# Block 0 of a feed-forward layer: second products of four more column tiles in three parts, and the low parts of five first weights made later, on VectorE

## The chip, the cores and the metric

The kernel runs on one core of a Trainium2 chip. The metric is the device time of one execution in microseconds (us): 551.14 for the kernel before, the median of three runs (551.05 to 551.84). Engines are named as in the profile: PE is TensorE (matmul), PEld its weight loads, DVE VectorE, ACT ScalarE, POOL GpSimd, and SP SyncE, whose queue issues most DMA transfers.

## What is computed

Three stages follow each other on 1536 tokens (2 batches of 768) of width 512. The change lies in the second.

```python
x = attention(q, k, v)                   # 8 heads of 64, window of 128 and 4 sink keys
h = x @ w_in                             # [1536, 512] @ [512, 2048]: the first products
g = np.maximum(0.01 * h, h)              # leaky ReLU
y = g @ w_out                            # [1536, 2048] @ [2048, 512]: the second products
...                                      # then a mixture of 8 experts, one per token
```

The weights `w_in` and `w_out` arrive as float64 and are turned into float32 on the chip, word by word.

## The kernel before, in words

**Blocks and column tiles.** The feed-forward layer takes the tokens in six blocks of 256 (two query tiles of 128 each), and the 2048 columns of `w_in` in 16 column tiles `f` of 128. For one block `j` and column tile `f`, `FFN.first` multiplies 128 columns of `w_in` with the block's `x` (`hps`, L1101), `FFN.leak` applies the leaky ReLU, and `FFN.second` adds `g` times 128 rows of `w_out` into two PSUM tiles `y`, one for each query tile (L1149). A product is written as a pair of column tile and kind: (f, 0) for the first weights, (f, 1) for the second.

**Two ways to multiply.** A product is made either of plain float32 operands, or "in parts": each operand is split into a rounded high part (ACT casts it: `wh` L1046, `gp` L1129) and the low rest (a subtraction on POOL or DVE: `wl` L1047, `gp` L1131), and three products are added: high by high, high by low, low by high. `FFN.in_parts` says which: every block after block 0 works in parts, and in block 0 the column tiles from `AHEAD[0]` (first products) and `AHEAD[1]` (second products) on. Before, `AHEAD = (5, 10)`.

**Block 0.** While block 0 runs, the weights are still arriving. Each column tile of weights is loaded by SP (`rawi`, `rawo`), and DVE converts it in three instructions (L1018 and L1022 write `word`, L1028 writes `cvt`, in pairs of column tiles). First all 16 first products run, then the second products of column tiles 0 to 13 (`LAG = 2`: the last two run in block 1). Attention for the following query tiles is woven between them. For a column tile in parts the function `ready` prepares the second product two column tiles ahead: the leaky ReLU's subtraction on POOL if it was put off (`gr` L1114, put off for `f >= LATE_G`), the split of the weights (`wh` on ACT, `wl` on POOL), the split of `g` (`gp` on ACT, then on POOL).

**Weights that block 0 used plain** must be split before block 1 needs them. The list `splits` holds them. Before, block 0 splits the first weights (f, 0) of column tiles 0 to 4 on POOL, one after each second product, and block 1 splits the ten second weights (f, 1) on DVE, `SPLIT = 1` for each column tile.

**What sets the order.** PE, SP, ACT, POOL, and up to the end of block 0 DVE too, keep the order in which the program issues their instructions; nothing is moved past a waiting instruction. Where DVE's conversions stand between other work is set by a planner (`Pace`), which compares its own sums of PE and DVE time (`pace.tensor`, `fill`). Tiles live in a pool of 70 slots, so an instruction that writes into a slot also waits for the last reader of the tile that held it.

**Saved weights.** The parts of column tiles 0, 1, 14 and 15 are written to a scratch buffer in HBM (`wscr`, L1057, on SP's queue) and read back in later blocks.

```python
def in_parts(self, j, f, x):
    return j > 0 or f >= self.ahead[x]
...
            self.late[f] = lambda: nc.gpsimd.tensor_tensor(out=g, in0=g, in1=r, op=ALU.subtract)
            if f < LATE_G:
                self.late.pop(f)()
```

Of the kernel before, what the change touches and what calls it, by code (L numbers as in the profile page):

```python
# [40 lines left out]

RAW = 5
LAG = 2
SPLIT = 1
LATE_G = 4
SLACK = 1.5
AHEAD = (5, 10)
WORD_US = 0.6
PARTS_US = 2.0
AFTER = range(9, 16)  # L50
# [901 lines left out]
class FFN:  # L952
# [12 lines left out]
    def __init__(self, nc, pools, A, xt, cap):  # L965
# [6 lines left out]
        self.w, self.v, self.raw, self.g, self.y = {}, {}, {}, {}, {}  # L972
        self.ahead, self.x0 = AHEAD, []
        self.seq = [(0, 0), (0, 1)] + [(f, x) for x in range(2) for f in range(1, self.NF)]
# [129 lines left out]
    def leak(self, j, f):  # L1104
# [3 lines left out]
        if j == 0:  # L1108
# [5 lines left out]
# [3 lines that stand above are left out]
# [898 lines left out]
def build(tc, A, n_sink, window, capacity):  # L2015
    nc = tc.nc
# [13 lines left out]
    with ExitStack() as es:  # L2030
# [34 lines left out]
        def step(*between):  # L2065

            nonlocal done
            d, pre, mid = steps.pop(0) if steps else (None, (), ())
            for f in (*pre, *between, *mid):
                f()  # L2070
            if d is not None:
                done = d
# [6 lines left out]
        if ring:  # L2079
# [3 lines left out]
            ffn = FFN(nc, p, A, xt, FFN.CAP)  # L2083
# [13 lines left out]
        if not ring:  # L2097
            pool(rawst, "raw", bufs=nraw, side="right")
            ffn = FFN(nc, p, A, xt, FFN.CAP - FEWER // 4)
# [18 lines left out]
        def some(calls, n):  # L2118
            for f in calls[:n]:
                f()  # L2120
            del calls[:n]
# [12 lines left out]
        def word():  # L2134

            if not conv:
                if chunk >= len(ffn.seq):
                    return False
                conv.extend(convert())
            f = conv.pop(0)  # L2140
            f()
            pace.dve += f.us
            if f.key:
                pace.ready[f.key] = pace.dve
            return True

        def fill():

            while started and pace.dve < pace.pe + SLACK and word():
                pass  # L2150
# [3 lines left out]
        def need(f, x):  # L2154

            while x not in ffn.v.get(f, ()) and x not in ffn.w.get(f, ()):
                word()
# [19 lines left out]
        pending, held, routing, splits, beside = [], [], [], [], []  # L2177
# [17 lines left out]
        def split(n, f=-1, x=0):  # L2195

            while splits and (n > 0 or f >= 0 and x not in ffn.w.get(f, ())):
                ffn.split(*splits.pop(0), nc.vector if ffn.phase > 1 else nc.gpsimd)
                n -= 1

        def second():
            j, f, i = pending.pop(0)
            if j == 0:
                need(f, 1)
                pace.tensor(*(1.4, (f, 1), PARTS_US) if ffn.in_parts(0, f, 1) else (1.88, (f, 1)))
            if j == 1:
                split(0, f, 1)
            last = i == ffn.NF - 1
            if j == late and i >= ffn.NF - HOLD:

                ffn.second(j, f, i == 0, last, range(TPB - 1))
                held.append((j, f, i))
                if last:
                    for t in range(TPB - 1):
                        rt.evac(j * TPB + t, ffn.y[j][t])
                return
            ffn.second(j, f, i == 0, last, range(TPB))
            del ffn.g[j, f]
            if j == 0:
                splits.extend([(f, 1)] * (not ffn.in_parts(0, f, 1)))  # L2220
            elif i < n_ev or j == late:
                del ffn.w[f]
            if j > 1 and i < n_ev:
                ffn.reload(ffn.order(j)[ffn.CAP + i])
            if last:
                ts = tuple(range(j * TPB, (j + 1) * TPB))
                for t, y in zip(ts, ffn.y.pop(j)):
                    rt.evac(t, y)
                routing.extend(route(ts, True) if j < late - 1 else late_route(ts))
                if j == late - 2 and rt.NU:  # L2230
                    routing.insert(-1, ex.rank)

        def ready(f):

            if f < ffn.NF:
                need(f, 1)
                if f in ffn.late:
                    ffn.late.pop(f)()
                if ffn.in_parts(0, f, 1):
                    ffn.split(f, 1, nc.gpsimd)  # L2240
                ffn.split_g(0, f)

        def block0():

            NF, last_t, ndone = ffn.NF, 2 * TPB - 1, 0
            pace.pe, pace.dve = 0.0, 1.7
            count = next((n + 1 for n, x in enumerate(steps) if x[0] == last_t), len(steps))
            for s in range(2 * NF - LAG):
                x, f = divmod(s, NF)
                if x == 0:  # L2250
                    need(f, 0)
                    ffn.first(0, f)
                    pace.tensor(*(1.42, (f, 0), PARTS_US) if ffn.in_parts(0, f, 0) else (1.95, (f, 0)))
                    if not ffn.in_parts(0, f, 0):
                        splits.append((f, 0))
                    ffn.leak(0, f)
                    if f == 0 and ffn.ahead[0] < NF:
                        ffn.split_x0()
                    fill()
                    for a in range(f + 2 if f else 0, f + 3):  # L2260
                        if ffn.ahead[0] <= a < NF:
                            need(a, 0)
                            ffn.split(a, 0, nc.gpsimd)
                    if f == NF - 1:
                        while conv:
                            word()
                        ffn.phase = 1
                        for a in range(LAG):
                            ready(a)
                else:  # L2270
                    pending.append((0, f, f))
                    second()
                    fill()
                    if f + LAG < NF - 1:
                        ready(f + LAG)
                    if splits and not splits[0][1]:
                        split(1)
                while ndone < min(count, max(1, count * (s + 1) // (2 * NF - LAG - 1))):
                    step()
                    ndone += 1  # L2280
                fill()
            while word():
                pass
            pending.extend((0, f, f) for f in range(NF - LAG, NF))
            ffn.store()
            ffn.phase = 2

        started = 1
        block0()
        order.close()  # L2290
        psc.close()
# [11 lines left out]
        for j in range(1, NB):  # L2303
# [14 lines left out]
            for i, f in enumerate(ffn.order(j)):  # L2318
# [10 lines left out]
                if (j, i) == (1, 0):  # L2329
                    ready(ffn.NF - 1)  # L2330
# [6 lines left out]
                while more():  # L2337
                    step()
                    ndone += 1
                split(SPLIT)  # L2340
                some(clears, rate)
# [87 lines left out]
```

## Time and profile before

| what | before |
| --- | --- |
| median of three runs | 551.14 us (551.05 to 551.84) |
| the profiled execution: its own time | 551.71 us |
| the profiled execution: its span, first to last instruction | 550.0 us |
| PE busy | 533.1 us, 97% of the span |
| DVE busy | 394.2 us, 72% |
| ACT busy | 291.6 us, 53% |
| POOL busy | 210.7 us, 38% |
| mean granted TensorE clock | 0.995 |

Busy time is an average over stages with different limits. Where an engine is nearly always busy, the question at each place is whether it waits, and for whom; where it is often idle, it can still be the one that the next step waits for. The rows for that stand in the section on rows; all lengths of time in them are us, except the mean of one instruction, in ns.

### The profile page before, as it was taken

Reading aid. Unit: us, or ns where it says so; the run is one execution under the profiler, and the core shown is the slowest. Engines: PE = TensorE matmul, PEld = TensorE weight load, DVE = VectorE, ACT = ScalarE, POOL = GpSimd, SP = SyncE. Lnnn points to the kernel's source line nnn. Section 1 sums busy time; section 2 is a strip of 40 time slices with the busy share of each in tenths; the row PEclk is TensorE's granted clock in tenths of the full one; section 3 lists DMA queues with packets and bytes.
Section 4 is the critical chain, followed back from the end, with each engine's and each line's share of the span. In section 5 each row is a group of like instructions: output and inputs, shape, how many; then the busy total and the mean of one; then the engine's idle time right before and its main releaser. Section 6 shows DMA issues by size and latency. Waiting matters only on the chain.

```text
span 550.0 us, 11107 instructions
## 1 busy us (share of the span) xinstructions
PE 533.1 (97%) x3653; PEld 457.9 (83%) x3653; DVE 394.2 (72%) x935; ACT 291.6 (53%) x858; POOL 210.7 (38%) x338
## 2 busy tenths in 40 slices
PE   8998999999999999999999999999999999999993
PEld 7777756888888888888888889888798988988782
DVE  5999996657439974898469952394587667838991
ACT  5768647765444454545454433373255545527771
POOL 6567579713525533553444552241110110102120
PEclk9999999999999999999999999999999999999998
DMA  9979873999564022420240037673376876747920
GB/s 226 243 226 283 258 268 99 360 276 324 170 225 116 21 57 66 129 56 22 68 128 28 1 113 237 217 228 124 99 215 214 254 243 191 241 130 227 348 81 7
DMA packets 83668, 93.72 MB, mean 170 GB/s; under 512 B 42963, under 2 KB 51155, under 8 KB 83472
## 3 DMA queue, kind: packets, MB, share of 16 engines
q1 hardware_dynamic: 81680, 87.78, 53.1%
q0 software_dynamic: 1920, 5.13, 2.6%
q8 instruction: 31, 0.51, 0.4%
q14 instruction: 37, 0.30, 0.2%
HBM read 74.10 MB, written 19.83 MB: 171 GB/s over the span
## 4 chain that ended last, share of the span: by engine, by line
PE 69%; DVE 14%; issue 8%; DMA 4%; POOL 2%; ACT 2%; POOLq 0%; ACTq 0%; DVEq 0%
PE y L1149 19%; PE hps L1101 19%; PE ph L1669 9%; PE py L1726 8%; DVE junk L1255 3%; DMA out<-ys,gt 3%; DVE word L1018 3%; PE ops L714 3%; DVE word L1022 2%; PE sps L618 2%; PE py L1732 1%; DVE cvt L1028 1%; DMA rawo<-in_moe_w_out 1%; PE pps L676 1%; DVE pm L628 1%
## 5 line engine op out<-in xcount | busy, mean ns | idle before, releaser
L1149 PE MATMUL y<-wh,gp 128*128 128x512 f32 x344 | 126.3, 408 | 0.2 <-POOL gp L1131 0.2
L1131 POOL TENSOR_TENSOR gp<-g,gp 128x256 fp32r<-128x256 f32 x77 | 68.0, 883 | 147.0 <-ACT gp L1129 124.8
L1101 PE MATMUL hps<-xth,wh 128*128 128x256 f32 x320 | 90.8, 284 | 0.0
L1101 PE MATMUL hps<-xtl,wh 128*128 128x256 f32 x320 | 90.4, 282 | 0.0
L1101 PE MATMUL hps<-xth,wl 128*128 128x256 f32 x320 | 90.0, 281 | 0.0
L1498 DVE TENSOR_TENSOR cw<-craw,cw 128x512 fp32r<-128x512 f32 x128 | 82.6, 690 | 4.4 <-ACT cw L1496 1.9
L1120 DVE TENSOR_TENSOR g<-hps,g 128x256 f32<-128x256 f32 x80 | 33.5, 419 | 60.9 <-ACT g L1119 60.7
L1149 PEld LDWEIGHTS y<-wh,gp 128*128 128x128 f32 x344 | 64.5, 188 | 14.7 <-POOL gp L1131 0.9
L1496 ACT CAST cw<-craw 128x512 fp32r<-128x512 f32 x112 | 63.5, 622 | 17.6 <-PE py L1732 9.2
L1149 PE MATMUL y<-wl,gp 128*128 128x512 f32 x172 | 67.6, 393 | 0.0
L1255 DVE SCALAR_TENSOR_TENSOR junk<-x,rows_of 128x512 f32<-128x512 f32 x48 | 62.9, 1311 | 1.2 <-ACT x L1227 1.0
L1101 PEld LDWEIGHTS hps<-xth,wh 128*128 128x128 f32 x320 | 60.3, 189 | 3.1 <-issue 0.4
L1101 PEld LDWEIGHTS hps<-xtl,wh 128*128 128x128 f32 x320 | 60.2, 188 | 2.7
L1119 ACT ACTIVATE g<-hps 128x256 f32<-128x256 f32 x80 | 30.5, 381 | 59.8 <-PE hps L1101 56.7
L1101 PEld LDWEIGHTS hps<-xth,wl 128*128 128x128 f32 x320 | 60.7, 190 | 0.0
L1726 PE MATMUL py<-cw,ht 128*128 128x512 f32 x216 | 53.7, 400 | 0.2 <-DVE ht L1714 0.2
L1129 ACT CAST gp<-g 128x256 fp32r<-128x256 f32 x80 | 32.7, 409 | 33.1 <-DVE g L1120 31.9
L1669 PEld LDWEIGHTS ph<-xt,cw 128*128 128x128 f32 x396 | 49.5, 189 | 0.7 <-issue 0.3
L1669 PE MATMUL ph<-xt,cw 128*128 128x256 f32 (+3 forms) x396 | 49.8, 287 | 0.1
L1726 PEld LDWEIGHTS py<-cw,ht 128*128 128x128 f32 x216 | 39.7, 188 | 9.4 <-DVE ht L1714 1.0
L1742 POOL DMA_INDIRECT out<-ys,gt x9 | 9.7, 1081 | 92.5 <-DVE ys L1741 92.5
L641 ACT ACTIVATE pm<-pm,mx 128x132 f32<-128x132 f32 (+1 forms) x80 | 31.8, 401 | 25.1 <-DVE mx L633 25.1
(264 smaller groups left out, 1024.6 us busy)
## 6 DMA issues: line engine op xcount, KB each, us to landing
craw<-in_moe_w SPq DMA_DIRECT2D x128, 256.0 KB
rawi<-in_moe_w_in SPq DMA_DIRECT2D x16, 512.0 KB
rawo<-in_moe_w_out SPq DMA_DIRECT2D x16, 512.0 KB
places<-zero SPq DMA_DIRECT2D x24, 257.0 KB
wh<-wscr SPq DMA_DIRECT2D x16, 256.0 KB
wl<-wscr SPq DMA_DIRECT2D x16, 256.0 KB
natv<-in_v SPq DMA_DIRECT2D x12, 256.0 KB
out<-zero SPq DMA_DIRECT2D x12, 256.0 KB
```

What stands on the lines that cost most here:

```text
L641: self.nc.scalar.activation(a, a, AF.Exp, bias=mx[:, pr, e:e + 1], accum_out=su[:, pr, e, 0:1])
L1101: nc.tensor.matmul(ps, lhsT=w, rhs=x, start=(n == 0), stop=(n == len(mm) - 1))
L1119: nc.scalar.activation(g, ps, AF.Copy, scale=0.01)
L1120: nc.vector.tensor_tensor(out=g, in0=ps, in1=g, op=ALU.max)
L1129: nc.scalar.copy(gp[:, 0], g)
L1131: eng.tensor_tensor(out=gp[:, 1], in0=g, in1=gp[:, 0].bitcast(F32), op=ALU.subtract)
L1149: nc.tensor.matmul(y, lhsT=l, rhs=r, start=(start and n == 0), stop=(stop and n == len(mm) - 1))
L1255: nc.vector.scalar_tensor_tensor(out=junk, in0=self.x2[ts[n]][:, 0:DM], scalar=1.0, in1=self.rows_of[:, :, e], op0=ALU.mult, op1=ALU.mult, ...
L1496: nc.scalar.copy(h, t)
L1498: eng.tensor_tensor(out=l, in0=t, in1=h.bitcast(F32), op=ALU.subtract)
L1669: nc.tensor.matmul(self.ph[f][:, sl], lhsT=self.w[e, "a", h, k][w][:, f * P:(f + 1) * P], rhs=self.xt[:, a, k, sl], start=(m == 0), stop=( ...
L1726: nc.tensor.matmul(self.py[n], lhsT=x, rhs=w, start=(h == 0 and f == 0 and m == 0), stop=(h == self.NH - 1 and f == self.HF - 1 and m == 2))
```

## The change

Five numbers and three places in the code:

- `AHEAD[1]` goes from 10 to 6: in block 0 the second products of column tiles 6 to 9 are made in parts too, so their weights and `g` are split in block 0 by `ready`.
- `LATE_G` goes from 4 to 9: the leaky ReLU's subtraction on POOL is put off for column tiles 9 to 15 alone; those of 4 to 8 follow their first products at once.
- Block 0 no longer splits first weights after its second products. At its end it splits two column tiles' (`EARLY_SPLITS = 2`) on DVE; block 1 splits the rest, two for each column tile (`SPLIT = 2`), ordered by when block 1 needs them.
- The second weights of column tile 15, prepared in block 1, get their low part on DVE and not on POOL.

```diff
-SPLIT = 1
-LATE_G = 4
+SPLIT = 2
+EARLY_SPLITS = 2
+LATE_G = 9
 SLACK = 1.5
-AHEAD = (5, 10)
+AHEAD = (5, 6)
...
                 if ffn.in_parts(0, f, 1):
-                    ffn.split(f, 1, nc.gpsimd)
+                    ffn.split(f, 1, nc.vector if ffn.phase > 1 else nc.gpsimd)
                 ffn.split_g(0, f)
...
                     if f + LAG < NF - 1:
                         ready(f + LAG)
-                    if splits and not splits[0][1]:
-                        split(1)
...
             ffn.store()
             ffn.phase = 2
+            splits.sort(key=lambda a: a[0] + LAG * a[1])
+            split(EARLY_SPLITS)
```

Three places of the built program show what moves. Line numbers of the changed kernel are one higher.

POOL's queue in the second half of block 0, before, from the masking of a probability tile (`pt`) on; `gr` is the leaky ReLU's subtraction, `wl` the low part of a weight tile, `gp` the low part of `g`, `pm` and `psk` scale attention's probabilities:

```order
L691 AFFINE_SELECT pt<-pt 128x512 x2
L1114 TENSOR_TENSOR gr<-gr 128x256 x3
L652 TENSOR_TENSOR pm<-pm,ri 128x528
L659 COPY psk_210<-pm 128x16
L1114 TENSOR_TENSOR gr<-gr 128x256
L1047 TENSOR_TENSOR wl<-cvt,wh 128x512
L1131 TENSOR_TENSOR gp<-gr,gp 128x256
```

The same place in the changed kernel, from the same `pt` to the same `gr`, `wl`, `gp`, which are those of column tile 10:

```order
L692 AFFINE_SELECT pt<-pt 128x512 x2
L1048 TENSOR_TENSOR wl<-cvt,wh 128x512
L1132 TENSOR_TENSOR gp<-gr,gp 128x256
L1048 TENSOR_TENSOR wl<-cvt,wh 128x512
L1132 TENSOR_TENSOR gp<-gr,gp 128x256
L1115 TENSOR_TENSOR gr<-gr 128x256
L1048 TENSOR_TENSOR wl<-cvt,wh 128x512
L1132 TENSOR_TENSOR gp<-gr,gp 128x256
L653 TENSOR_TENSOR pm<-pm,ri 128x528
L660 COPY psk_210<-pm 128x16
L1115 TENSOR_TENSOR gr<-gr 128x256
L1048 TENSOR_TENSOR wl<-cvt,wh 128x512
L1132 TENSOR_TENSOR gp<-gr,gp 128x256
```

Two `gr` (column tiles 7 and 8) have left this stretch, and three `wl` and three `gp` (column tiles 7, 8 and 9) have come into it. The rest of block 0 on POOL is the same in both: for column tiles 11, 12 and 13 `gr`, `wl`, `gp`, with two `pt` ahead of 13.

ACT's queue at the end of block 0 in the changed kernel, from the parts of column tile 14 on (`xth` is the high part of attention's result, `g` the first step of block 1's leaky ReLU):

```order
L1047 CAST wh<-cvt 128x512
L1130 CAST gp<-gr 128x256
L723 CAST xth<-ops 128x2x128
L1047 CAST wh<-cvt 128x512 x2
L1120 ACTIVATE g<-hps 128x256
```

Before, `g` follows `xth` at once. The two `wh` between them are those of the first weights of column tiles 0 and 1, with which block 1 begins. DVE's queue at the same place in the changed kernel:

```order
L592 TENSOR_TENSOR kTl_132<-qps,kTh_131 128x2x128
L734 TENSOR_TENSOR xtl<-ops,xth 128x2x128
L1048 TENSOR_TENSOR wl<-cvt,wh 128x512 x2
L1121 TENSOR_TENSOR g<-hps,g 128x256
```

The two `wl` are the low parts of the same two weights; before, `g` follows `xtl`.

## Rows read from the trace of the kernel before

**Rows 1.** Four stretches of the span: busy time and instructions of each engine.

```profile
core 0: us, PE busy (x) PEld busy (x) DVE busy (x) ACT busy (x) POOL busy (x), PEclk, DMA share, GB/s
34.65:59.80 25.15, 21.34 (x175) 18.47 (x174) 25.05 (x53) 19.01 (x63) 17.84 (x18) 1.00 0.93 279
76.65:95.66 19.01, 18.83 (x112) 11.34 (x110) 14.84 (x32) 11.68 (x39) 16.46 (x22) 1.00 0.50 147
95.66:107.40 11.74, 11.69 (x80) 10.37 (x81) 7.43 (x18) 9.47 (x32) 8.91 (x13) 1.00 0.97 353
```

**Rows 2.** Chain that ended last, by time: start, us, engine, tile, line.

```profile
65.62 5.97 DMA rawo<-in_moe_w_out
...
94.93 0.74 POOL gp L1131
95.71 1.20 PE y L1149 x4
96.91 1.53 PE hps L1101 x12
...
111.18 1.36 PE y L1149 x6
```

**Rows 3.** PE's timeline; in brackets idle time before, and its releaser.

```profile
68.23 3.70 PE L1149 MATMUL y<-cvt,gr 128*128 128x512 f32 x8
71.86 0.39 PE L618 MATMUL sps<-kTh,qT 64*128 64x264 f32 x2
...
96.74 0.28 PE L1101 MATMUL hps<-xth,wh 128*128 128x256 f32 x1
...
98.16 0.28 PE L1101 MATMUL hps<-xth,wl 128*128 128x256 f32 x1
```

**Rows 4.** POOL's timeline in the second half of block 0.

```profile
76.65 1.23 POOL L691 TENSOR_SCALAR_AFFINE_SELECT pt<-pt 128x512 f32<-128x512 f32 x2 [0.48 <-ACT pt L688]
77.85 2.12 POOL L1114 TENSOR_TENSOR gr<-gr 128x256 f32<-128x256 f32 x3
82.44 1.07 POOL L652 TENSOR_TENSOR pm<-pm,ri 128x528 f32<-128x528 f32 x1 [2.48 <-DVE ri L650]
...
87.22 1.29 POOL L1047 TENSOR_TENSOR wl<-cvt,wh 128x512 fp32r<-128x512 f32 x1
88.47 0.73 POOL L1131 TENSOR_TENSOR gp<-gr,gp 128x256 fp32r<-128x256 f32 x1
89.17 0.73 POOL L1114 TENSOR_TENSOR gr<-gr 128x256 f32<-128x256 f32 x1
...
94.93 0.73 POOL L1131 TENSOR_TENSOR gp<-gr,gp 128x256 fp32r<-128x256 f32 x1
95.61 0.75 POOL L1114 TENSOR_TENSOR gr<-gr 128x256 f32<-128x256 f32 x1
```

**Rows 5.** ACT's timeline, around the same places.

```profile
76.96 0.64 ACT L697 ACTIVATE sp<-kps,of_pair 128x128 f32<-128x128 f32 x2
...
96.39 0.41 ACT L1129 CAST gp<-gr 128x256 fp32r<-128x256 f32 x1 [0.39 <-POOL gr L1114]
96.70 0.37 ACT L722 CAST xth<-ops 128x256 fp32r<-128x256 f32 x1
...
101.27 0.62 ACT L1046 CAST wh<-cvt 128x512 fp32r<-128x512 f32 x1
```

**Rows 6.** Low parts on DVE up to 130 us, as a group.

```profile
L1047 DVE TENSOR_TENSOR wl<-cvt,wh 128x512 fp32r<-128x512 f32 x8 | 7.1, 889 | 3.8 <-ACT wh L1046 3.7
```

**Rows 7.** Two of them in DVE's timeline.

```profile
101.92 1.20 DVE L1047 TENSOR_TENSOR wl<-cvt,wh 128x512 fp32r<-128x512 f32 x1 [0.95 <-ACT wh L1046]
...
105.46 0.69 DVE L1047 TENSOR_TENSOR wl<-cvt,wh 128x512 fp32r<-128x512 f32 x1 [0.81 <-ACT wh L1046]
```

**Rows 8.** POOL's timeline beside the first of the two.

```profile
101.83 0.75 POOL L1131 TENSOR_TENSOR gp<-gr,gp 128x256 fp32r<-128x256 f32 x1
102.53 1.20 POOL L1131 TENSOR_TENSOR gp<-g,gp 128x256 fp32r<-128x256 f32 x1
```

## The prediction, made before the changed kernel ran

> **What bounds the kernel now.** PE is busy 97% of the span, so the first question is where it waits. I read the stretches first, then the chain of waits, then the timelines of the engines named there.
>
> In the second half of block 0, from 76.65 to 95.66 us, PE is busy 18.83 of 19.01 us, which looks like a bound by PE; but POOL is busy 16.46 us there too, and its only long gap is 2.48 us ahead of the scaling `pm`, where it waits for DVE's `ri` [rows 1, 4]. The chain of waits says who is last at the end of that stretch: it comes from DVE and a late load (`rawo`), runs through POOL, and reaches PE at 95.71 with POOL's `gp`, the low part of column tile 13; from there on it is PE after PE [rows 2]. So at the end of block 0 PE and POOL finish almost together, POOL a little later. After that, from 95.66 to 107.40, PE is busy 11.69 of 11.74 us [rows 1]: nothing there takes up a delay, and what block 0 ends later, the kernel ends later. In the first half of block 0 DVE, with its conversions, is the bound: 25.05 of 25.15 us between 34.65 and 59.80 [rows 1].
>
> **The change, part by part.**
>
> *PE's work.* Two plain second products (column tiles 2 and 3) take from 68.23 to 71.86, 1.81 us for each [rows 3]; one in parts takes 1.36 us on the chain [rows 2]. Four column tiles change over: 4 x (1.81 - 1.36) = 1.8 us less work for PE. It counts only if nobody is later than PE.
>
> *POOL's work in the stretch that ends block 0.* The order of instructions shows three `wl` and three `gp` (column tiles 7, 8, 9) that come in between `pt` at 76.65 and the `gp` of column tile 13, and two `gr` (7 and 8) that leave. From start to start a `wl` takes 1.25 us (87.22 to 88.47), a `gp` 0.70 (88.47 to 89.17), a `gr` 2.12 / 3 = 0.71 [rows 4]. That is 3 x 1.25 + 3 x 0.70 - 2 x 0.71 = 4.4 us more. None of it can start before `pt`: `pt` waits for ACT, and the `wh` of column tile 7 stands in ACT's queue behind the two `sp` of 76.96, so it ends near 78.1, some 0.3 us after POOL is free again at 77.85 [rows 4, 5]. Against it, the gap of 2.48 us ahead of `pm` is filled, since `ri` is asked for only after all this. Net: 4.4 + 0.3 - 2.5 = **2.2 us**. The `gp` of column tile 13 ends near 97.9 where it ended at 95.66. PE waits for it: its saved 1.8 us turn into waiting, as PE needs the `gp` of column tiles 10 to 13 in turn and POOL makes one set in gr + wl + gp = 2.66 us where PE uses it up in 1.36. The bounds of this term: 1.4 us if 5% of POOL's 16.5 us are overstated (the page calls its spans rough), 2.5 us if no gap is filled better than I reckon and the wait of 0.3 us doubles.
>
> *The first weights of block 1.* Before, column tiles 0 and 1 were split on POOL long before block 1. Now ACT's `wh` for them stands behind `gp` and `xth`, in order, and that `gp` waits for the `gr` of column tile 14, which POOL makes after the `gp` of column tile 13. On the rows of before, with POOL's `gp` ending at 95.66: `gr` until 96.36, ACT's `gp` at 96.39, `xth` at 96.70 [rows 4, 5]. Then one `wh` from about 97.0, 0.62 us long [rows 5], and the `wl` on DVE from about 97.7. The first product of block 1 needs this `wl` for its third of twelve matmuls, which then take (98.16 - 96.74) / 11 = 0.13 us apiece [rows 3]. A `wl` on DVE has a mean of 0.89 us [rows 6], so: 97.7 + 0.89 + 10 x 0.13 = 99.9, where it ended at 98.3: **1.6 us** on top of the first term. The bounds come from two rows: 0.69 us for an undisturbed `wl` gives 1.4, 1.20 us for one that POOL disturbs gives 1.9 [rows 7].
>
> Which of the two to expect is a question of who else reads SBUF. The `wl` of 1.20 us began at 101.92, while POOL's `gp` ran from 101.83; POOL's next `gp`, at 102.53, took 1.20 instead of about 0.73 us [rows 4, 7, 8]. The Trainium skill, SBUF — State Buffer, section Who interferes with whom, says that a VectorE instruction with two SBUF inputs and a GpSimd instruction that reads SBUF exclude each other for a whole instruction. The rows agree for part of an instruction each. By the rule the new `wl`, which would come up just as POOL begins the `gp` of column tile 14, waits that out, 0.73 + 0.69 = 1.4 us, and the sum would be 0.5 us higher than mine.
>
> *The rest.* The five `gr` moved forward are 3.5 us of POOL between 34.65 and 59.80, where POOL has 25.15 - 17.84 = 7.3 us free and DVE is the bound [rows 1]: 0; without that room they would cost up to 3.5. The five `wl` taken from POOL before 76.65 were waited for by nobody: 0. In block 1 DVE makes twelve low parts instead of ten, and two per column tile early on, so that some five more fall into its first five column tiles: 5 x 0.89 = 4.4 us, against 11.74 - 7.43 = 4.3 us that DVE has free between 95.66 and 107.40 [rows 1], with more after it. I take 0; if each were disturbed, 5 x 1.20 - 4.3 = 1.7 us. ACT's casts only change places. SP's queue reads the same in both; its stores of column tiles 0 and 1 wait longer, and what stands behind them, clears and a load of `v`, shifts with block 1: 0.
>
> **Sum.** 2.2 + 1.6 = 3.8 us, on the profiled execution's own 551.71 us: 555.5. That execution was 0.57 us above the median of 551.14, so as a median **555.0 us**. What a measurement of this kernel can tell from no change is about 0.2%, 1.1 us.
>
> **The rivals.**
>
> *Faster: PE sets the end of block 0.* Then 4 x 0.45 = 1.8 us are won: 549.4 us. For it speaks that PE is busy 18.83 of 19.01 us in that stretch, more than POOL [rows 1]. It decides from the point where POOL hands over the `gp` of column tile 13 by 95.66 - 1.8 = 93.9, which is 4.0 us earlier than I reckon, and where the `wh` and `wl` of block 1 are early too. Against it speaks that POOL's queue is a plain sum of rows. Chance 0.10.
>
> *Only POOL's term.* If ACT and DVE reach the first weights of block 1 before PE does, say because the `gr` of column tile 14 holds up less than its order says, only 2.2 us stay: 553.4 us. Chance 0.20.
>
> *DVE too full in block 1.* Pairs of low parts stand ahead of the leaky ReLU's `g`, for which PE's second products wait two column tiles later. With the 1.7 us from above: 556.7 us. Against it: those two column tiles of PE's work lie between. Chance 0.15.
>
> *No change.* A smaller overrun on POOL and the PE time won on the way cancel out: about 551 us. That needs both terms to be wrong by half. Chance 0.08.
>
> **How the numbers follow.** My forecast, both terms, has 0.47; its own range is 553.9 to 555.5 (1.4 + 1.4 to 2.5 + 1.9 on 551.1). With the two other slower cases that makes 0.82 for slower, 0.10 for faster, 0.08 for the same. The range 552.3 to 557.0 takes in the three slower cases with the bounds of their terms; the faster case and no change stay outside.
>
> **What would show it.** Right: in the profile after, POOL has no gap of over 1 us between 77.9 and 97; PE waits for POOL's `gp` and `wl` from column tile 10 to 13, with several us in all; the first L1102 product of block 1 starts near 99 and waits first for ACT's `wh`, then for DVE's `wl`; from about 102 on every product of block 1 comes 3.8 us later than before. Wrong: if PE goes through column tiles 10 to 13 without waits, the first term falls; if block 1's first product runs through in 1.5 us, the second falls; if gaps on PE appear between 105 and 120 with DVE's `g` as releaser, the DVE rival is at work.

## The result, and the profile after

The changed kernel takes 559.09 us (median of four runs, 559.04 to 560.26) beside 551.31 us for the kernel before on the same chip: ratio 1.0143, 95% interval 1.0131 to 1.0155. It is 7.8 us slower. Forecast were 3.8 us, and a range that ended at 557.0: the direction was right, the size half of what came. The two profiled executions differ by 7.0 us of span; the one before the change was 0.4 us above its median.

| what | before | after |
| --- | --- | --- |
| the profiled execution: its own time | 551.71 us | 559.04 us |
| its span | 550.0 us | 557.0 us |
| PE busy | 533.1 us, 97% | 536.0 us, 96% |
| DVE busy | 394.2 us, 72% | 397.5 us, 71% |
| POOL busy | 210.7 us, 38% | 212.2 us, 38% |
| mean granted TensorE clock | 0.995 | 0.992 |

PE is busy 2.9 us longer, although it has 1.8 us less to do. The page's row of the granted clock, 40 slices of 13.9 us, shows where to look: the eighth slice, 97.5 to 111.4 us, has a 7.

```profile
PEclk9999999799999999999999999999999999999999
```

Two of the stretches of [rows 1] for the kernel after, behind shorter ones from 100 to 108 us:

```profile
core 0: us, PE busy (x) PEld busy (x) DVE busy (x) ACT busy (x) POOL busy (x), PEclk, DMA share, GB/s
...
100.00:101.00 1.00, 0.00 (x0) 0.00 (x0) 1.00 (x1) 0.00 (x0) 0.94 (x2) 0.73 1.01 385
101.00:102.00 1.00, 0.60 (x3) 0.60 (x4) 0.96 (x2) 0.00 (x0) 0.92 (x3) 0.50 0.31 119
102.00:107.00 5.00, 5.00 (x25) 4.25 (x25) 2.03 (x6) 2.27 (x8) 0.83 (x3) 0.50 0.41 157
107.00:108.00 1.00, 1.00 (x6) 0.82 (x5) 1.00 (x2) 1.00 (x3) 1.00 (x2) 0.85 0.62 242
76.65:95.66 19.01, 17.42 (x114) 11.97 (x113) 13.87 (x29) 11.86 (x37) 18.64 (x23) 1.00 0.54 171
95.66:107.40 11.74, 9.02 (x43) 6.64 (x40) 6.74 (x14) 6.21 (x20) 7.43 (x10) 0.71 0.39 149
```

In block 0's second half POOL is now full (18.64 of 19.01 us) and PE has slack. Behind it, from 101 to 107 us, PE runs at a granted clock of 0.50, the 1.2 GHz level, where it stood at 1.00, the 2.4 GHz level, before.

The chain of waits from 95 us on names every step; [rows 2] has it for the kernel before:

```profile
95.18 0.53 POOL wl L1048
...
96.42 0.72 POOL gp L1132
97.15 0.70 POOL gr L1115
...
97.87 0.03 ACT gp L1130
...
98.19 0.36 ACT xth L723
98.55 0.53 ACT wh L1047
...
99.17 2.18 DVE wl L1048
...
101.40 2.50 PE hps L1102 x10
103.90 1.62 PE sps L619 x9
105.52 2.42 PE y L1150 x6
107.94 1.42 PE hps L1102 x12
```

And PE's own timeline at the head of block 1; [rows 3] has the first product of before:

```profile
99.12 0.39 PE L1102 MATMUL hps<-xth,wh 128*128 128x256 f32 x1 [0.71 <-ACT wh L1047]
99.34 0.28 PE L1102 MATMUL hps<-xtl,wh 128*128 128x256 f32 x1
101.40 0.58 PE L1102 MATMUL hps<-xth,wl 128*128 128x256 f32 x1 [1.77 <-DVE wl L1048]
101.78 0.42 PE L1102 MATMUL hps<-xth,wh 128*128 128x256 f32 x1
...
107.78 0.28 PE L1102 MATMUL hps<-xth,wh 128*128 128x256 f32 x1
```

The `wl` on DVE, from 99.17 to 101.35, lies beside two instructions of POOL:

```profile
99.04 0.72 POOL L1132 TENSOR_TENSOR gp<-gr,gp 128x256 fp32r<-128x256 f32 x1
99.73 1.06 POOL L653 TENSOR_TENSOR pm<-pm,ri 128x528 f32<-128x528 f32 x1
```

The span's 7.0 us lie between these rows. Four steps make them up, each against the rows of before:

1. POOL's `gp` of column tile 13 begins at 96.42, before at 94.93: **+1.5 us**.
2. The third matmul of block 1's first product begins at 101.40. Before, it began at 96.74 + 2 x 0.12 = 96.98; that is +4.4 us, so 2.9 us come on top of POOL's. Of these 1.6 us are the late `wh` and a `wl` of 0.89 us, as forecast;
3. and 2.18 - 0.89 = **1.3 us** are the `wl` that took 2.18 us.
4. From that matmul to the next first product it takes 107.78 - 101.40 = 6.38 us. The next one began at 100.78 before, 3.80 us behind the third matmul: **+2.6 us**, in the stretch at half the clock, where a matmul of this shape lasts 0.41 instead of 0.28 us.

1.5 + 1.6 + 1.3 + 2.6 = 7.0.

### The profile page after: what moved, and what is told of

Its sections match the earlier page's. It is cut to its first block, busy times and chain, and to the rows that moved or that the text cites. A ratio compares the mean times of both kernels' runs of the same rounds, so it can differ in the third digit from the quotient of the medians.

```text
span 557.0 us, 11158 instructions
## 1 busy us (share of the span) xinstructions
PE 536.0 (96%) x3661; PEld 461.2 (83%) x3661; DVE 397.5 (71%) x937; ACT 292.9 (53%) x862; POOL 212.2 (38%) x340
## 4 chain that ended last, share of the span: by engine, by line
PE 53%; issue 18%; DVE 12%; DMA 10%; POOL 3%; ACT 2%; SPq 0%; another core or an unknown queue 0%; POOLq 0%; ACTq 0%; DVEq 0%
PE y L1150 20%; PE hps L1102 19%; DMA out<-ys,gt 9%; DVE junk L1256 3%; PE ops L715 3%; PE sps L619 3%; DVE word L1019 2%; DVE word L1023 1%; DVE cvt L1029 1%; PE pps L677 1%; POOL wl L1048 1%; PE qps L566 1%; PE py L1727 1%; PE ph L1698 1%; PE sps L877 1%
## 5 line engine op out<-in xcount | busy, mean ns | idle before, releaser
L1150 PE MATMUL y<-wh,gp 128*128 128x512 f32 x360 | 133.3, 411 | 1.4 <-POOL gp L1132 1.1
L1150 PEld LDWEIGHTS y<-wh,gp 128*128 128x128 f32 x360 | 67.7, 189 | 18.1 <-POOL gp L1132 2.7
L1150 PE MATMUL y<-wl,gp 128*128 128x512 f32 x180 | 71.3, 396 | 0.4 <-POOL wl L1048 0.3
```

The costliest lines, as they stand in the source:

```text
L1150: nc.tensor.matmul(y, lhsT=l, rhs=r, start=(start and n == 0), stop=(stop and n == len(mm) - 1))
```

## The experiments

Ten runs of nine kernels (e10 is e6 again), most of them small edits of the changed kernel. Times are medians; the ratio is to the kernel before, which ran beside them on the same chip (551.16 us for the first four, 551.59 for the next four, 551.57 for the last two).

| kernel | us | ratio, 95% interval |
| --- | --- | --- |
| e1: only the first weights moved | 556.66 | 1.0094, 1.0078 to 1.0109 |
| e2: only the second products in parts | 555.06 | 1.0069, 1.0056 to 1.0083 |
| e3: change, early first weights on POOL | 553.53 | 1.0043, 1.0029 to 1.0056 |
| e4: change, PE kept busy during its wait | 556.91 | 1.0096, 1.0082 to 1.0109 |
| e5: e3, and late `gr` early | 550.38 | 0.9974, 0.9964 to 0.9985 |
| e6: change, late `gr` early | 551.70 | 1.0013, 0.9996 to 1.0030 |
| e7: before, late `gr` early | 551.79 | 0.9998, 0.9990 to 1.0007 |
| e8: change, early first weights on DVE within block 0 | 556.59 | 1.0081, 1.0066 to 1.0096 |
| e9: e5, two more second products in parts | 550.71 | 0.9983, 0.9974 to 0.9992 |
| e10: e6 again, one execution | 554.11 | |

### The two halves of the change, each alone

The first weights alone (e1):

```diff
-LATE_G = 9
+LATE_G = 4
-AHEAD = (5, 6)
+AHEAD = (5, 10)
```

> The second products as before (split in two from column tile 10 on), only the first weights moved: block 1's first two at block 0's end, on ACT and VectorE. Theory (most of the loss is the late first weights: the wait for them on PE, the locked-out low part on VectorE and the half clock behind it): POOL's gp of column tile 13 ends near 95.6 us as before, the first product of block 1 still waits for ACT's wh and VectorE's wl, the granted clock falls to about 0.5 behind it; the loss of the change less POOL's 1.5 us, so 556 to 558 us. Rival (POOL's chain of block 0 is the cause, and the late weights only follow it): 551.3 us, clock 1.00.

It was 5.5 us slower than before, as expected, with the wait for `wl` and the clock's fall as in the changed kernel. PE's timeline, then one window, where the clock was 1.00 before [rows 1]:

```profile
98.02 0.39 PE L1102 MATMUL hps<-xth,wh 128*128 128x256 f32 x1 [0.71 <-ACT wh L1047]
...
100.30 0.58 PE L1102 MATMUL hps<-xth,wl 128*128 128x256 f32 x1 [1.77 <-DVE wl L1048]
```

```profile
95.66:107.40 11.74, 9.05 (x40) 7.08 (x40) 7.66 (x14) 6.21 (x19) 7.43 (x10) 0.71 0.41 156
```

The second products alone, with the early first weights split on POOL as before (e2):

```diff
-SPLIT = 2
-EARLY_SPLITS = 2
+SPLIT = 1
+EARLY_SPLITS = 0
...
+                    if splits and not splits[0][1]:
+                        split(1)
...
-            splits.sort(key=lambda a: a[0] + LAG * a[1])
```

> The second products in three parts from column tile 7 on, the first weights prepared as before, within the second products on POOL. Theory: block 1's first weights lie ready, PE does not wait for them, the granted clock stays 1.00 from 95 to 108 us, and POOL's chain costs 1.5 us, up to 2.7 with the early low part that POOL keeps behind column tile 6: 552.5 to 554 us. Rival (POOL's chain alone makes the loss): 558 to 559 us.

3.9 us slower, with the clock at 1.00 from 95.66 to 107.40: the direction as expected, the size 1 us above the range, since POOL's `gp` of column tile 13 came at 98.18, 3.2 us later than before. So each half alone costs several microseconds, and neither is the whole.

### The early first weights, and the clock

In e3 the early first weights go back to POOL, where it stands idle at 66 us:

```diff
                         ready(f + LAG)
+                    if f < EARLY_SPLITS:
+                        split(1)
...
-            split(EARLY_SPLITS)
```

> The changed kernel, but the first two first weights of block 1 are prepared on POOL behind second products 0 and 1 of block 0. Theory: the wait for wl is gone, the granted clock stays at 1.00, POOL's 1.5 us are left: about 552.8 us. Rival (something else of the moved work makes the loss): above 556 us.

2.4 us slower than before: the wait and the clock's fall are gone (1.00 from 95.66 to 107.40), and 5.4 of the 7.8 us with them. What is left is POOL's term, 97.13 - 94.93 = 2.2 us, just as forecast:

```profile
97.13 0.74 POOL L1132 TENSOR_TENSOR gp<-gr,gp 128x256 fp32r<-128x256 f32 x1
```

In e4 PE gets something to do while it waits:

```diff
             split(EARLY_SPLITS)
+            busy = p["ps"].tile([P, P], F32, tag="att", name="busy")
+            for n in range(13):
+                nc.tensor.matmul(busy, lhsT=ident, rhs=ident, start=True, stop=True)
```

> The changed kernel with 13 further 128 by 128 matmuls of the identity, whose result nobody reads, on PE at block 0's end, where it waits for block 1's first weights. If the clock falls because PE stood idle there: granted clock near 1.00 from 101 to 107 us, and the 2.58 us between the third matmul of the first product and the next first product are given back: about 556.5 us. If the clock has another cause: 559.1 us or more, clock still about 0.5.

It loses 5.75 us where the change loses 7.8, so it saves 2.0 us by the medians (2.6 by the ratios), although nothing that the kernel needs was done earlier. The windows show the clock, the timeline (the 13 matmuls, each of them two entries) the next first product 106.20 - 102.40 = 3.80 us behind the third matmul, as before the change:

```profile
99.00:103.00 4.00, 4.00 (x35) 3.88 (x34) 3.20 (x3) 1.60 (x4) 3.85 (x5) 1.00 0.51 197
103.00:107.00 4.00, 4.00 (x33) 3.46 (x32) 2.66 (x7) 2.95 (x10) 1.59 (x4) 1.00 0.61 232
```

```profile
99.25 3.06 PE L2290 MATMUL busy<-ident 128*128 128x128 f32 x26
...
102.40 0.39 PE L1102 MATMUL hps<-xth,wl 128*128 128x256 f32 x1
...
106.20 0.28 PE L1102 MATMUL hps<-xth,wh 128*128 128x256 f32 x1
```

So the clock of the changed kernel fell because PE stood idle: with PE busy in the same place it does not. The slow stretch is the price of the wait, for the most part paid after it.

### POOL's queue

In e5 to e7 the late `gr` of POOL are issued at the end of block 0's first products, where POOL stands idle some 4 us; e5 has e3's edit too, e6 is the changed kernel with this alone, e7 the kernel before with this alone.

```diff
                         ffn.phase = 1
+                        for late_f in range(LATE_G, NF - 1):
+                            ffn.late.pop(late_f)()
```

> Both repairs at once: block 1's first two first weights on POOL behind second products 0 and 1, and the six late gr subtractions (column tiles 9 to 14) at the end of the first products, where POOL stands idle some 4 us. Theory (POOL's queue is what is left of the loss): gp of column tile 13 ends 5 x 0.69 = 3.45 us earlier than in the run with the early weights on POOL (97.87), at about 94.4 us, PE becomes the bound again, and its four saved 0.45 us show: 549.5 to 550.3 us, faster than the kernel before. Rival (the arrival or conversion of the second weights paces this stage): 551 us or more.

0.26% faster than before, 1.2 us by the medians, so 9.0 us better than the change, each taken beside its own kernel before. The only kernels here that beat both are this one and e9, made from it. POOL's `gp` of column tile 13 ends at 95.18, not at 94.4, because a load (`rawo`) held DVE 1.40 us at 72.7 in this execution; PE is busy 18.84 of 19.01 us again:

```profile
76.65:95.66 19.01, 18.84 (x125) 13.43 (x124) 16.87 (x36) 15.45 (x50) 18.52 (x22) 1.00 0.57 170
95.66:107.40 11.74, 11.74 (x85) 10.48 (x84) 7.90 (x15) 8.19 (x27) 6.48 (x11) 1.00 0.83 309
```

> The kernel before with its late gr subtractions (column tiles 4 to 14) at the end of the first products. Theory: PE is the bound of block 0's second half before the change (busy 18.83 of 19.01 us), so a shorter POOL chain gives at most those 0.2 us: 550.8 to 551.3 us. Rival (POOL's chain was the bound already): 549.5 us or less.

No difference, as expected. The run alone does not settle it, since the eleven `gr` in one piece hold up a `pt` for which PE waits 1.22 us at 68.42. The rows of before do: PE is busy 18.83 of 19.01 us [rows 1], so a shorter chain of POOL had no more than 0.2 us to give there.

> The changed kernel with only the six late gr subtractions moved to the end of the first products; the first weights of block 1 stay at block 0's end. Theory: POOL's chain is short, but PE still waits for ACT's wh and VectorE's wl at the head of block 1 and the clock still falls to about 0.5 behind that wait: 554.5 to 557 us, at least 4 us over the run with both repairs. Rival (the late weights only follow POOL's late chain): below 552 us.

A miss: the median lies where the rival had it. The late first weights cost only 1.3 us more than in e5, where 4 were expected, and the times scatter: twelve runs from 550.49 to 555.19 us, beside 549.76 to 551.73 in e5. Without the wait for `gr`, ACT's `gp` and the `wh` behind it come in time (PE waits for no `wh` any more), and the rest hangs on the `wl` alone. The first profile was of an execution of 550.55 us, so the kernel ran again for a second profile (e10):

> The same kernel as the run with the early gr and the late first weights, for a second profile, since its twelve times lie between 550.5 and 555.2 us and the first profile was of one of the shortest. If the long ones are the wait at block 1's head: with a time above 553 us the profile shows PE waiting 1 us or more for wl there and a granted clock below 1.00 behind it; with a time near 550.5 us a wait of about 0.4 us and clock 1.00.

This execution took 554.11 us. The two profiles hold the same program; they part at one instruction. First the short one, its chain, then POOL's and PE's timelines:

```profile
94.23 0.91 DVE wl L1048
...
95.19 0.87 PE hps L1102 x5
```

```profile
93.29 1.29 POOL L1048 TENSOR_TENSOR wl<-cvt,wh 128x512 fp32r<-128x512 f32 x1
94.55 1.17 POOL L1132 TENSOR_TENSOR gp<-gr,gp 128x256 fp32r<-128x256 f32 x1
95.68 1.51 POOL L653 TENSOR_TENSOR pm<-pm,ri 128x528 f32<-128x528 f32 x1
...
95.19 0.39 PE L1102 MATMUL hps<-xth,wl 128*128 128x256 f32 x1 [0.38 <-DVE wl L1048]
```

Then the long one, with its windows at the end:

```profile
95.24 2.64 DVE wl L1048
...
97.92 1.23 PE hps L1102 x7
```

```profile
94.32 1.29 POOL L1048 TENSOR_TENSOR wl<-cvt,wh 128x512 fp32r<-128x512 f32 x1
95.58 0.71 POOL L1132 TENSOR_TENSOR gp<-gr,gp 128x256 fp32r<-128x256 f32 x1
96.26 1.06 POOL L653 TENSOR_TENSOR pm<-pm,ri 128x528 f32<-128x528 f32 x1
...
97.92 0.39 PE L1102 MATMUL hps<-xth,wl 128*128 128x256 f32 x1 [2.08 <-DVE wl L1048]
```

```profile
97.00:98.00 1.00, 0.07 (x1) 0.08 (x1) 1.00 (x2) 0.00 (x0) 0.88 (x2) 1.00 0.84 320
98.00:99.00 1.00, 1.00 (x8) 1.00 (x9) 0.48 (x1) 0.00 (x0) 0.98 (x2) 0.86 0.30 117
99.00:102.00 3.00, 3.00 (x18) 2.44 (x18) 1.17 (x5) 1.37 (x6) 0.26 (x1) 0.50 0.60 226
102.00:103.00 1.00, 1.00 (x6) 0.82 (x5) 0.96 (x4) 1.00 (x4) 0.21 (x1) 0.93 0.00 0
```

In both, DVE's `wl` begins some 0.35 us ahead of the end of a POOL `wl`. In the short execution, by the lengths, it gets its turn when that ends, and POOL's next two instructions are the longer ones (1.17 and 1.51 instead of 0.72 and 1.07 us). In the long one POOL's `gp` and `pm` go first, at their undisturbed lengths, and DVE's `wl` stands 2.64 us. The wait of PE is 1.7 us longer, the clock falls to 0.50 behind it, and the span grows by 3.6 us (548.4 to 552.0); some 1.0 us of that was there before, as the first product began at 95.45 and not at 94.41. Of the other times of this kernel there is no profile: that they part at the same instruction is likely, not shown.

### The same subtraction in the middle of block 0

In e8 the two early low parts are made on DVE beside POOL's unbroken chain:

```diff
+                    if 8 <= f < 8 + EARLY_SPLITS:
+                        ffn.split(*splits.pop(0), nc.vector)
...
-            split(EARLY_SPLITS)
```

> The changed kernel with block 1's first two first weights prepared on VectorE behind second products 8 and 9 of block 0, in the middle of POOL's unbroken chain. If a subtraction of VectorE is held up by POOL's work beside it: each wl takes 1.2 us or more there, as it took 2.18 us at the head of block 1; if not, 0.6 to 0.7 us as the ones of block 1 beside an idle POOL. The time either way, since nothing waits for them: 553 to 554 us, clock 1.00.

A miss in the time and the clock, and telling. The two `wl` took 0.71 and 0.76 us there, so this time it was POOL that lost: its `gp` beside them took 1.17 and 1.19 us instead of 0.74. And something did wait: ACT's `gp` waits for POOL's `gr`, the early `wh` stands behind it, DVE's queue behind the `wh`, and PE behind an `xtl` in that queue. One row each from the timelines of ACT, DVE (two) and PE, then the windows:

```profile
87.11 0.41 ACT L1130 CAST gp<-gr 128x256 fp32r<-128x256 f32 x1 [2.70 <-POOL gr L1115]
...
88.14 0.71 DVE L1048 TENSOR_TENSOR wl<-cvt,wh 128x512 fp32r<-128x512 f32 x1 [4.61 <-ACT wh L1047]
88.78 0.41 DVE L734 TENSOR_TENSOR xtl<-ops,xth 128x256 fp32r<-128x256 f32 x1
...
89.25 0.39 PE L619 MATMUL sps<-kTh,qT 64*128 64x264 f32 x1 [3.72 <-DVE xtl L734]
```

```profile
90.00:91.00 1.00, 1.00 (x4) 0.75 (x4) 0.97 (x5) 1.00 (x5) 0.48 (x2) 0.63 0.00 0
91.00:92.00 1.00, 1.00 (x4) 0.81 (x3) 0.96 (x4) 0.58 (x2) 1.00 (x1) 0.50 0.03 8
```

A work item without a reader nearby can still stop one: it stands in a queue ahead of work that has a reader. The clock fell here too, behind a wait of 3.72 us.

### Two more products in parts

The last edit is made on e5:

```diff
-AHEAD = (5, 6)
+AHEAD = (5, 4)
```

> The run with both repairs, and two more second products of block 0 (column tiles 4 and 5) in three parts, whose low parts fall where POOL stands idle 5 us (70 to 75 us in that run). If PE bounds block 0's second half: 2 x 0.45 = 0.9 us less, about 0.2% under the run with both repairs (550.4 us beside a kernel before of 551.6). If the conversion and arrival of the second weights pace the stretch from 60 to 76 us: no gain, or a loss of up to 1.5 us where POOL's chain is pushed back.

550.71 us, no gain on e5. In its profile PE is busy 16.40 of 16.85 us from 59.80 to 76.65 and 18.31 of 19.01 after it, so it waits 0.7 us in the second stretch, where it waited 0.2 in e5's. Whether the saved 0.9 us went there is not shown, since the profile of e5 has a wait of its own for the late load, 1.17 us at 73.76.

## Why the forecast was right in direction and wrong in size

- **PE's 1.8 us** were won and lost in waiting, as forecast: PE is busy 17.42 of 19.01 us. e5 wins 1.2 us, so most of them can be had.
- **POOL's term, 2.2 us:** 1.5 us in the profiled execution, where the load behind `rawo` came in time and POOL's stage began 0.8 us earlier, 2.2 us in e3, where DVE waited 0.53 us for it. The sum of rows held: from `pt` to the `gp` of column tile 13 it took 18.28 us before, 20.57 after and 20.54 in e3, 2.3 us more in both. The waits forecast from column tile 10 to 13 are there, but only of 0.2 to 0.4 us each and 1.6 us in the whole stretch, where several were forecast.
- **The first weights of block 1, forecast +1.6 us: the step that failed.** Its order of events was right to the instruction: `gr`, ACT's `gp`, `xth`, `wh`, then `wl` on DVE, the product waiting at its first and third matmul. But the `wl` was taken at 0.89 us, with 1.20 as the upper bound, and took 2.18: 1.3 us too little. By its end it stood through two POOL instructions, `gp` (99.04) and `pm` (99.73). The twelve traces together say how such a `wl` waits. On DVE they hold 131 `wl` of this shape: 40 met no instruction of POOL and took 0.68 to 0.69 us. Of the 91 that did, 85 end 0.54 to 0.55 us behind the end of a POOL instruction (the other six took 0.67 to 0.68 us). In 81 of the 85 this is the instruction that ran when the `wl` began. The four that let one or two more go first are the first `wl` at the head of block 1 in the changed kernel, e1, e4 and e10; e6's, at the same place, is not among them. So the wait is for whole POOL instructions, nearly always one, and the mean of eight between 0.69 and 1.20 us was no guide to it.
- **The rule on the shared port** (the Trainium skill, SBUF — State Buffer, section Who interferes with whom) gave 1.4 us, by one POOL instruction waited out. It was the better guide than my mean, and the 81 `wl` agree with it; at this place it was still short of 2.18. The section also says that the order of issue decides who blocks. In e6 and e10 the order is the same, POOL's `wl`, DVE's `wl`, POOL's `gp`: e6 agrees (0.91 us), while in e10 two POOL instructions that came up later went first (2.64 us). There the measurement decides: the turn is not settled by the order alone.
- **A term left out, the other step that failed:** 2.6 us for the granted clock. The forecast let PE wait at the head of block 1 and priced the wait at its own length. In its place the runs show 2.48 us of waiting, and then a stretch at 0.50 that costs 2.6 us more. e4 gives that term back with PE busy; e10 and e8 show it behind other waits. From the forecast's 3.8 us to the span's 7.0: less 0.7 at POOL, 1.3 more at the `wl`, 2.6 more for the clock.
- **What was taken at 0 held.** The five `gr` moved forward cost nothing, and from 108 to 160 us PE waits for nobody: the rival in which DVE is too full in block 1 didn't come up. Two other rivals came about by repairs: with the first weights early only POOL's term stays (e3, 553.53 us, forecast 553.4), and with both repairs PE sets the end of block 0 (e5).

The two halves do not add. With the weights late and POOL's chain long the loss is 7.8 us, with either one mended 2.4 (e3) and 0.1 (e6), with both -1.2 (e5): ACT's `gp` carries POOL's delay to the `wh`, the turn between DVE and POOL decides about the `wl`, and the clock adds to what waiting remains. Why DVE misses its turn at the head of block 1, and in e6 does not, stays open: the two profiles of the same program begin the `wl` within 0.02 us of the same place relative to POOL's `wl`, and taking that apart was not tried.

## What to carry to other kernels

A wait of PE can cost more than its length, here 2.48 us of waiting and 2.6 us behind it: read the granted clock in the windows behind a wait, and ask whether something can keep PE busy. Before moving work to an engine that looks idle, follow what its instruction will wait for on every queue it passes, and what stands behind it there. And cost an instruction from the rows of its kind that had the same neighbours running, not from the mean of its group; where it must share with a neighbour that works without a pause, give a range: here the rest of one POOL instruction in 81 cases of 85, and 0.91 and 2.64 us from one program.

## What the runs showed that was not expected

- The slow stretch does not coincide with the wait. In the changed kernel PE waited 0.71 and 1.77 us up to 101.40; the clock fell within the second wait (0.73 from 100 to 101), stayed at 0.50 to 107 us although PE was busy from 101.40 on, and was 1.00 from 108 on. In e10 the fall followed a single wait of 2.08 us and came after PE had resumed, and the 0.50 lasted some 3 us, from 99 to 102. Waits of 0.38 us (e6) and 1.17 us (e5) left the clock at 1.00.
- Two executions of one program, with the same queues, differ by 3.6 us of span, of which some 2.6 us follow the turn of a single DVE instruction.
- A DVE subtraction of 0.69 us lasted up to 2.64 us beside POOL, and POOL's `gp` of 0.72 up to 1.20: either side can lose.
